# An adaLN block with linear attention and a token-mixing MLP: q's shift row is made from a folded sum in one matmul, an iteration later

## The chip, the cores and the metric

The kernel runs on one core of one Trainium2 chip. The metric is the device time of one execution in microseconds, taken as the median of several runs; the kernel before took 433.37 us (three runs, 433.33 to 433.41). All lines named L... are lines of the kernel before, unless the text says "after".

## The reference

Only the part that the change touches is shown; x has 2048 rows (tokens) of D = 448 channels, there are 16 heads of 28 channels, everything is float32.

```python
mod = (silu(c) @ w_mod).reshape(6, 448)
sa, ca, ga, sb, cb, gb = mod
h = layernorm(x) * (1 + ca) + sa
qkv = h @ wqkv                       # q, k, v: (2048, 448) each
phi = lambda t: where(t > 0, t + 1, exp(t)) + 1e-6
kv = sum over tokens of phi(k)^T v;  z = sum over tokens of phi(k)
o = phi(q) @ kv / (phi(q) @ z + 1e-6)          # per head
x = x + ga * (o @ wo)
h = layernorm(x) * (1 + cb) + sb
x = x + gb * transpose(gelu(transpose(layernorm(h)) @ w1 + b1) @ w2 + b2)
```

## The kernel before, in words

The 2048 tokens are cut into NT = 16 tiles of 128. Phase A computes k, phi(k), the sums over tokens, and some of the q's; phase B makes the attention's output and the MLP's first product; phase C the second. The change lies in phase A alone.

**Two-part numbers.** TensorE's fast type is a rounded float (F32R), so a float32 operand is split into a high part (ScalarE copies it into F32R) and a low part (VectorE, or a GpSimd transfer that adds, makes the rest), and a product is the sum of high x high, high x low and low x high.

**q and k without a normalised x.** For j = 0 (q) and j = 1 (k), the weights are multiplied by (1 + ca) per channel (Whi and Wlo, `w_high` L260 and `w_low` L272). x itself is used unnormalised, transposed (hh and hl, L411 and L415). The mean and the shift sa come in through two rows of each matrix: the negative column sum of the scaled weights, which is multiplied by a token's mean, and the row sa @ W, which is multiplied by its standard deviation (the spread is divided out later, in the exponent's scale). Both rows are rows of the tile Wrow[j] from partition 64 up, each in a high and a low part; `close(t, j)` (L439) ends a tile's product with one matmul over them. So no q can be closed before q's Wrow[0] is complete.

**How the row is made.** `row_part(0, ch)` (L278, L280) sums sa * W over four chunks of channels into accb, 128 partitions x 448, on VectorE. `row_sum(0)` (L287) lays the column sums of seven weight tiles into a PSUM tile rowb with seven F32R matmuls with the selector sel_s. `row_bias(0)` (L290) adds accb's sum over partitions with one matmul with the selector sel_b; accb and sel_b are plain float32, which the profile records as two matmuls. `row_out(0)` takes rows 64 to 97 out of PSUM on ScalarE (L294) and makes the low parts on VectorE (L295). The same is done for k (j = 1) far earlier.

**The loop and its order.** The order on each engine is the order in which the code issues: there is no reordering, each engine has its own queue and waits in it for what it needs. The loop `for t in range(4, NT)` (L682) is one iteration for each token tile: TensorE projects tile t + 1 for k, closes tile t, adds tile t - 4 into the sums of phi(k)^T x (`a_outer`, cacc, L554), transposes two tiles' mean and deviation rows on odd t (`a_transpose`, rw, L404), and from t = 10 on projects a q tile (`a_q`, L432 and L439 with the name qp). ScalarE and VectorE follow with the exponentials (L446, L449), the copies of the transposed rows (`a_copy`, L407), the splits and the norms (L496, L500, L505, L506). `a_pk_parts` (L527, L528) makes the low part of phi(k) for most tiles by a copy on ScalarE and an accumulating GpSimd transfer; `sum_end` (L541) issues another accumulating transfer. GpSimd's pow (L352) makes the deviations. SyncE's queue loads the tiles. In the kernel before, row_sum(0) and row_bias(0) stand in iteration 9 behind the close of tile 9, and row_out(0) at that iteration's end.

The modulation vectors use a like step: `mod_add(j)` (L237) folds partitions 64 to 111 onto the first ones, `mod_high(j)` (L242, L243) splits the folded 64 partitions into one tile, high part in partitions 0 to 63 and low part in 64 to 127.

Work tiles of phase A come from one ring of 74 slots (`slot`): each new tile takes the place of an old one and waits until that has been read.

Of the kernel before, what the change touches and what calls it, by code (L numbers as in the profile page):

```python
# [8 lines left out]
F32 = mybir.dt.float32  # L9
F32R = mybir.dt.float32r  # L10
AF = mybir.ActivationFunctionType
ALU = mybir.AluOpType
AX = mybir.AxisListType

P = 128
S, D, F = 2048, 448, 1792
# [15 lines left out]
ROWS = 98  # L32
# [19 lines left out]
def block_kernel(ctx: ExitStack, tc: tile.TileContext, x, xt, wqkv, wo, w1, b1, w2, c, wmod, wfirst, out):  # L52
    nc = tc.nc
# [5 lines left out]
    cst = ctx.enter_context(tc.tile_pool(name="cst", bufs=1))  # L59
# [16 lines left out]
    def moving(new, name, dt=F32R, parts=P):  # L76
        return new(name, dt=dt, parts=parts, w=512)[:, 16:16 + D]

    def bank(name):
        return psum.tile([P, 512], F32, name=name, tag="bank")  # L80
# [19 lines left out]
        nc.gpsimd.affine_select(out=m3, in_=m3, compare_op=ALU.is_ge, fill=0.0, base=DH - 1,  # L100
                                pattern=[[0, 4], [DH, 4], [0, DH]], channel_multiplier=-1)

    cst.tile([P, 112], F32, name="space")
    mhalf = cst.tile([P, 2], F32, name="mhalf")
    nc.vector.memset(mhalf, -0.5)
    roots = cst.tile([P, 2], F32, name="roots")
# [2 lines left out]
    sel_b = cst.tile([P, ROWS], F32, name="sel_b")  # L109
# [3 lines left out]
    for i in (64, 66, 96):  # L113
        nc.gpsimd.memset(sel_f[:, i:i + 1], -1.0)
        nc.gpsimd.memset(sel_b[:, i + 1:i + 2], 1.0)
    sel_s = cst.tile([P, ROWS], F32R, name="sel_s")
    rowst = []
    for i in range(RING):
        rowst.append(cst.tile([P, P], F32R, name=f"rowst{i}"))
# [115 lines left out]
    def mod_add(j):  # L235
        acc = macc[j]
        nc.vector.tensor_add(acc[:G - 64], acc[:G - 64], acc[64:])  # L237

    def mod_high(j):
        acc, both = macc[j], moving(slot, f"mh{j}")  # L240
        macc[j] = (both,)
        nc.scalar.activation(both[:64], acc[:64], AF.Copy)  # L242
        return lambda: nc.vector.tensor_sub(both[64:], acc[:64], both[:64].bitcast(F32))  # L243
# [12 lines left out]
    Whi, Wlo, Wrow, rowb, accb = {}, {}, {}, {}, {}  # L256
# [26 lines left out]
    def row_sum(j):  # L283
        rowb[j] = bank(f"rowb{j}")
        ws = [Whi[j, ch] for ch in range(4)] + [Wlo[j, ch] for ch in range(3)]
        for i, w in enumerate(ws):
            nc.tensor.matmul(rowb[j][:ROWS, :D], sel_s, w, start=(i == 0), stop=False)  # L287

    def row_bias(j):
        nc.tensor.matmul(rowb[j][:ROWS, :D], sel_b, accb.pop(j), start=False, stop=True)  # L290

    def row_out(j):
        ps, w = rowb.pop(j), Wrow[j]
        nc.scalar.activation(w[64:ROWS], ps[64:ROWS, :D], AF.Copy)  # L294
        nc.vector.tensor_sub(w[96:ROWS], ps[96:ROWS, :D], w[96:ROWS].bitcast(F32))  # L295
# [105 lines left out]
    def a_transpose(t):  # L401
        ps = bank(f"rw{t}")
        tps[t], tps[t + 1] = ps[:ROWS - 64, :P], ps[64:ROWS, :P]
        nc.tensor.transpose(ps[:ROWS, :P], rowst[t // 2 % RING][:, :ROWS].bitcast(F32), ident)  # L404
# [29 lines left out]
    def project(t, j, name):  # L434
        projects([(t, kind, ch) for ch in range(3) for kind in ("hh", "wl", "hl")] + [(t, "hh", 3)], j, name)

    def close(t, j):
        ps = pps.pop((t, j))
        nc.tensor.matmul(ps[:, :D], heads[t][1][:ROWS, 384:], Wrow[j][:ROWS], start=False, stop=True)  # L439
        return ps[:, :D]  # L440
# [10 lines left out]
    def a_exp(t, ps):  # L451
        a_exp1(t, ps)
        a_relu(t, ps)
# [22 lines left out]
    def a_q(t):  # L476
        project(t, 0, "qp")
        qps[t] = close(t, 0)
        del heads[t]
# [5 lines left out]
    def a_phi_q(keep=0):  # L485
        a_exp_q(keep)
        for t in sorted(eqs):
            pq[t] = phi_q(t)
# [24 lines left out]
    def a_pk_high(t):  # L513
        pks[t] = (moving(slot, f"pkh{t}"), moving(slot, f"pkl{t}"))
        nc.scalar.activation(pks[t][0], pkf[t], AF.Copy, bias=1e-6)

    def a_pk_parts(t):
        if t not in pks:
            a_pk_high(t)
        a_pk_low(t)  # L520

    def a_pk_low(t):
        pk, (hi, lo) = pkf.pop(t), pks[t]
        if t in DVE_LOW:
            nc.vector.scalar_tensor_tensor(lo, pk, 1e-6, hi.bitcast(F32), op0=ALU.add, op1=ALU.subtract)
        else:
            nc.scalar.activation(lo, hi.bitcast(F32), AF.Copy, scale=-1.0, bias=1e-6)  # L527
            nc.gpsimd.dma_start(lo, pk, accum_op=ALU.add)  # L528
        if t < 2:
            pksum.append(pk)  # L530
        elif t in SUM_DMA:
            late_sum.append((pksum[t % 2], pk))
        else:
            nc.vector.tensor_add(pksum[1], pksum[1], pk)
# [10 lines left out]
    def a_outer(t):  # L545
        if not cacc:
            cacc.extend(bank(f"cacc{ch}") for ch in range(4))
        xh, xl = xss.pop(t)
        kh, kl = pks.pop(t)
        for ch in range(4):  # L550
            s = slice(ch * P, (ch + 1) * P)
            todo = [(xh, kh), (xh, kl)] + ([(xl, kh)] if ch < 3 else [])
            for i, (a, b) in enumerate(todo[::1 if t > 1 else 2]):
                nc.tensor.matmul(cacc[ch][:, :D], a[:, s], b, start=(t == 0 and i == 0),  # L554
                                 stop=(t == NT - 1 and i == len(todo) - 1))
        if t < 2:
            for ch in range(4):
                nc.tensor.matmul(cacc[ch][:, :D], xh[:, ch * P:(ch + 1) * P], kl, start=False, stop=False)
# [121 lines left out]
    wo_sb = []  # L680
    late = [t for t in range(NT) if t not in Q_EARLY.values()]
    for t in range(4, NT):  # L682
        if 5 < t < NT - 1:
            project(t + 1, 1, "kp")
        kp = close(t, 1) if t > 4 else kps[4]
        if t == 9:
            row_sum(0)
            row_bias(0)
        if t > 4:
            a_outer(t - KV_LAG)  # L690
        if t % 2 and 4 < t < NT - 2:
            a_transpose(t + 1)
        if t in Q_EARLY:
            a_q(Q_EARLY[t])
        if t == 12:
            mp = mod_sum2(2)
        pair = t % 2 and 7 < t + 3 < NT
        if pair:
            first, second, end = a_stats_dve((t + 3, t + 4))
            first(0)  # L700
        if 5 <= t < 9:
            w_low(0, t - 5)
        if pair:
            second(0)
        if 5 <= t < 9:
            row_part(0, t - 5)
        a_phi_q(t in Q_EARLY)
        if t == 9:
            a_exp(t, kp)
        if t % 2 and 4 < t < NT - 2:  # L710
            a_copy(t + 1)
            a_copy(t + 2)
        if t != 9:
            a_exp(t, kp)
        if 7 < t + 3 < NT:
            a_split_high(t + 3)
        a_pk_parts(t - 1)
        highs = HIGH_AT.get(t, (t - 2,))
        for i in highs[:1]:
            a_norm(i)  # L720
            a_high(i)
        if t % 2 == 0 and 4 < t < NT - 3:
            low = a_rows(t + 2)
        if t == 11:
            low2 = mod_high(2)
        for j, i in MOD_AT.get(t, ()):
            mod_add(j) if i is None else mod_part(j, i)
        if t == 14:
            low4()
        a_pk(t, kp)  # L730
        if t % 2 == 0 and 4 < t < NT - 3:
            low()
        if 7 < t + 3 < NT:
            a_split_low(t + 3)
        for i in highs[1:]:
            a_norm(i)
            a_high(i)
        if pair:
            first(1)
        for i in highs:  # L740
            a_low(i)
        if pair:
            second(1)
            end()
        sum_end()
        if 4 <= t < 8:
            w_high(0, t - 4)
            if t == 7:
                w_row(0)
        if t == 9:  # L750
            row_out(0)
        if t == 12:
            mod_out(2, mp)
            make_mask()
        if t in FETCH:
            load_xt(FETCH[t])
            load_x(FETCH[t])
        if 7 <= t < 11:
            mod_part(2, t - 7)
        if t == 10:  # L760
            mod_add(2)
        if t == 11:
            low2()
        if t == 13:
            low4 = mod_high(4)
        if t in (7, 10):
            load_mod(4 if t == 7 else 3)
        if t == 10:
            load_qkv(2, tslot)
        if t == 8:  # L770
            for g in range(4):
                w = tslot(f"wo{g}", parts=G)
                nc.sync.dma_start(w, wo[g * G:(g + 1) * G, :])
                wo_sb.append(w)
            b12 = cst.tile([P, NF + NT], F32, name="b12")
            nc.sync.dma_start(b12, b1)
            b1c, b2c = b12[:, :NF], b12[:, NF:]
        if t >= 13:
            nc.vector.tensor_mul(wo_sb[t - 13], wo_sb[t - 13], mods[2][:G])
        load_to(PRE_LOAD.get(t, 0))  # L780
# [34 lines left out]
    for ch in range(4):  # L815
        for g in range(4):
            s = slice(g * G, (g + 1) * G)
            nc.tensor.matmul(kvb[:G, s], raw_w[2, ch][:, s], csum[ch][:, s], start=(ch == 0 and g == 0),  # L818
                             stop=(ch == 3), skip_group_check=True)
# [168 lines left out]
    for i in range(NT + LAG):  # L988
# [11 lines left out]
        t = i - LAG  # L1000
# [292 lines left out]
    for o0, n in W1G[1:]:  # L1293
# [5 lines left out]
        for r in range(first, NT):  # L1299
# [5 lines left out]
            if xleft:  # L1305
                t = xleft.pop(0)
# [80 lines left out]
```

## Time and profile before

| | |
|---|---|
| median of three runs | 433.37 us (433.33 to 433.41) |
| the profiled execution | 434.09 us, span 432.4 us |
| granted clock of TensorE | 1.00 |
| TensorE busy | 427.9 us, 99% of the span |
| VectorE, ScalarE, GpSimd busy | 365.1, 278.9, 120.1 us |
| DMA between 44 and 72 us | full (a share of 1.00 of the 16 engines), 240 GB/s |

The profile is one execution. In its lists an operation is named by the tile that it writes and those that it reads (out<-in); "idle before" is the time that its engine stood just before it, with what ended the wait. A matmul's 0.36 us is its whole way through the array; matmuls that follow each other start every 0.20 us, which the chain of work shows. The iteration with t = 9 lies between about 46 and 58 us: on TensorE its last matmuls end at 53.5 us, on VectorE its last operation starts at 57.42 us.

### The profile page before, as it was taken

How to read it: one execution, taken by the hardware profiler on the slowest of the kernel's cores; microseconds unless marked ns; L12 is line 12 of the kernel's file. 1: busy time of each engine (PE TensorE's matmuls, PEld its weight loads, DVE VectorE, ACT ScalarE, POOL GpSimd, SP SyncE). 2: the span in 40 equal slices, each digit the busy share in tenths (PEclk: the TensorE clock that was granted, in tenths of full speed). 3: DMA queues.
4: the chain of work that ended last, by engine and by line, in shares of the span. 5: the costliest groups of instructions: out<-in, count | busy, mean ns of one | idle time of the engine just before them, and what ended most of it. 6: DMA issues, size and time to landing. Idle time of an engine off the chain costs nothing.

```text
span 432.4 us, 7216 instructions
## 1 busy us (share of the span) xinstructions
PE 427.9 (99%) x2331; PEld 398.0 (92%) x2331; DVE 365.1 (84%) x814; ACT 278.9 (65%) x595; POOL 120.1 (28%) x199
## 2 busy tenths in 40 slices
PE   8999999999999999999999999999999999999997
PEld 8888899999899999999999999999999999999996
DVE  4899987889899999998579695739799998898894
ACT  5799869658578899996755263537464664655550
POOL 4345444300026577775200000010113131132010
PEclk9999999999999999999999999999999999999999
DMA  8997997565300036354427461577379977986431
GB/s 282 385 337 162 239 264 162 89 206 193 86 1 0 26 74 148 74 125 97 145 85 244 142 212 50 166 203 210 79 193 214 207 159 159 214 170 144 85 46 41
DMA packets 63797, 66.14 MB, mean 153 GB/s; under 512 B 4816, under 2 KB 55312, under 8 KB 63760
## 3 DMA queue, kind: packets, MB, share of 16 engines
q1 hardware_dynamic: 54688, 50.90, 37.8%
q0 software_dynamic: 8784, 14.32, 20.8%
q10 hardware_dynamic: 288, 0.46, 0.4%
q8 instruction: 18, 0.29, 0.3%
q14 instruction: 19, 0.16, 0.1%
HBM read 46.30 MB, written 7.34 MB: 124 GB/s over the span
## 4 chain that ended last, share of the span: by engine, by line
PE 97%; DVE 1%; ACT 1%; issue 0%
PE y L1183 19%; PE up L951 10%; PE up L950 10%; PE up L952 10%; PE y L1184 9%; PE cacc L554 7%; PE qp L432 7%; PE op L893 7%; PE kp L432 6%; PE op L900 1%; PE warm L188 1%; PE tq L863 1%; PE qp L439 1%; PE kvb L818 1%; PE wp L968 1%; PE rowb L287 1%
## 5 line engine op out<-in xcount | busy, mean ns | idle before, releaser
L950 PE MATMUL up<-h2h,ph 128*128 128x448 f32 x224 | 81.2, 362 | 0.0
L951 PE MATMUL up<-h2l,ph 128*128 128x448 f32 x224 | 81.2, 362 | 0.0
L952 PE MATMUL up<-h2h,pl 128*128 128x448 f32 x224 | 80.8, 361 | 0.0
L1138 POOL DMA_DIRECT2D a<-a x16 | 14.2, 964 | 142.6 <-DMA pr<-in_B_w_dram 76.7
L950 PEld LDWEIGHTS up<-h2h,ph 128*128 128x128 f32 x224 | 42.0, 188 | 3.1
L952 PEld LDWEIGHTS up<-h2h,pl 128*128 128x128 f32 x224 | 41.9, 187 | 3.0
L951 PEld LDWEIGHTS up<-h2l,ph 128*128 128x128 f32 x224 | 42.0, 188 | 2.3
L84 DVE TENSOR_TENSOR pl<-pr,ph 128x512 fp32r<-128x512 f32 x46 | 30.7, 688 | 2.6 <-ACT ph L83 1.7
L1189 ACT ACTIVATE cc<-y 128x448 f32<-128x448 f32 x24 | 13.0, 546 | 26.7 <-PE y L1184 26.7
L1102 DVE TENSOR_TENSOR u<-u,mod 128x448 f32<-128x448 f32 x14 | 8.7, 623 | 23.0 <-ACT u L1101 22.8
L83 ACT ACTIVATE ph<-pr 128x512 fp32r<-128x512 f32 x46 | 27.6, 623 | 0.8 <-PE up L952 0.5
L1101 ACT ACTIVATE u<-up,b 128x448 f32<-128x448 f32 x14 | 8.8, 625 | 25.4 <-PE up L952 24.9
L432 PE MATMUL kp<-wh,hh 128*128 128x448 f32 x64 | 23.8, 377 | 0.0
L554 PE MATMUL cacc<-pkh,xh 128*128 128x448 f32 x64 | 23.6, 369 | 0.0
L432 PE MATMUL qp<-wh,hh 128*128 128x448 f32 x64 | 23.5, 368 | 0.0
L1203 POOL DMA_DIRECT2D out_dram<-yt x14 | 12.7, 909 | 37.3 <-DVE yt L1194 27.9
L843 POOL TENSOR_SCALAR den<-den 128x16 f32<-128x16 f32 x16 | 8.8, 548 | 44.2 <-DVE den L840 44.2
L554 PE MATMUL cacc<-pkl,xh 128*128 128x448 f32 x56 | 20.3, 362 | 0.0
L893 PE MATMUL op<-wph,pth 128*128 128x448 f32 x48 | 18.7, 390 | 0.0
L1144 DVE TENSOR_TENSOR a<-a,s 128x512 f32<-128x512 f32 (+1 forms) x32 | 18.5, 622 | 0.0
L83 ACT ACTIVATE s2h<-s 128x512 fp32r<-128x512 f32 (+1 forms) x16 | 8.3, 569 | 15.5 <-DVE s L1144 15.5
L1183 PE MATMUL y<-ub,a11h 128*128 128x448 f32 x56 | 18.2, 375 | 0.0
(235 smaller groups left out, 1383.7 us busy)
## 6 DMA issues: line engine op xcount, KB each, us to landing
pr<-in_B_w_dram SPq DMA_DIRECT2D x56, 256.0 KB, 3.1
a<-in_B_w_dram SPq DMA_DIRECT2D x32, 256.0 KB, 4.8
a<-in_B_w_dram SPq DMA_DIRECT2D x32, 192.0 KB, 4.7
xt<-in_xt_dram SPq DMA_DIRECT2D x16, 256.0 KB, 5.0
x<-in_A_x_dram SPq DMA_DIRECT2D x16, 224.0 KB, 5.0
wm<-in_B_wmod_dram SPq DMA_DIRECT2D x16, 196.0 KB, 5.2
out_dram<-x SPq DMA_DIRECT2D x14, 224.0 KB, 2.3
out_dram<-yt POOLq DMA_DIRECT2D x14, 224.0 KB, 6.1
```

The source lines that it names most:

```text
L83: nc.scalar.activation(hi, full, AF.Copy)
L84: nc.vector.tensor_sub(lo, full, hi.bitcast(F32))
L432: nc.tensor.matmul(pps[t, j][:, :D], a[:, ch * P:(ch + 1) * P], w, start=first, stop=False)
L554: nc.tensor.matmul(cacc[ch][:, :D], a[:, s], b, start=(t == 0 and i == 0), stop=(t == NT - 1 and i == len(todo) - 1))
L893: nc.tensor.matmul(opb[t][:, :D], a, b, start=(ch == n == 0), stop=False)
L950: nc.tensor.matmul(ps[:, :D], hi[:, sl], mh, start=first, stop=False)
L951: nc.tensor.matmul(ps[:, :D], hi[:, sl], ml, start=False, stop=False)
L952: nc.tensor.matmul(ps[:, :D], lo[:, sl], mh, start=False, stop=last)
L1138: nc.gpsimd.dma_start(w, a, accum_op=ALU.add)
L1144: nc.vector.tensor_tensor(w, raw2[q, a][i], raw2[q, b][i], op=op)
L1183: nc.tensor.matmul(ps[:, :D], h[:, s], w, start=opens and r == 0, stop=False, skip_group_check=True)
L1184: nc.tensor.matmul(ps[:, :HD], l[:, s], wh, start=False, stop=closes and r == PAIRS - 1, skip_group_check=True)
```

## The change

q's row (j = 0) is made in another way; k's is left as it was.

- In iteration 9, behind `a_pk_parts(8)`, a GpSimd transfer adds accb's upper 64 partitions onto its lower 64 (`accum_op` add, 64 x 448).
- At the end of iteration 9, where row_out(0) stood, the new `row_fold(0)` copies sel_b into an F32R tile sel_r (ScalarE), copies the folded sum into the lower half of a new tile rb0 (ScalarE), and writes the low part into its upper half (VectorE).
- row_sum(0) and row_bias(0) go from iteration 9, behind the close of tile 9, to the very start of iteration 10. row_bias(0) takes sel_r and rb0, both F32R, in one matmul. row_out(0) goes to behind the close of tile 10.
- mod_add(2) goes from the end of iteration 10 to iteration 11, just ahead of mod_high(2).
- The tile "space" gives up the columns that sel_r takes. rb0 is one slot more in the ring.

```diff
-    cst.tile([P, 112], F32, name="space")
+    cst.tile([P, 14], F32, name="space")
...
+    sel_r = cst.tile([P, ROWS], F32R, name="sel_r")
...
     def row_bias(j):
-        nc.tensor.matmul(rowb[j][:ROWS, :D], sel_b, accb.pop(j), start=False, stop=True)
+        nc.tensor.matmul(rowb[j][:ROWS, :D], sel_r if j == 0 else sel_b, accb.pop(j), start=False, stop=True)
+
+    def row_fold(j):
+        acc, both = accb[j], moving(slot, f"rb{j}")
+        nc.scalar.activation(sel_r, sel_b, AF.Copy)
+        nc.scalar.activation(both[:64], acc[:64], AF.Copy)
+        nc.vector.tensor_sub(both[64:], acc[:64], both[:64].bitcast(F32))
+        accb[j] = both
...
     for t in range(4, NT):
+        if t == 10:
+            row_sum(0)
+            row_bias(0)
         if 5 < t < NT - 1:
             project(t + 1, 1, "kp")
         kp = close(t, 1) if t > 4 else kps[4]
-        if t == 9:
-            row_sum(0)
-            row_bias(0)
+        if t == 10:
+            row_out(0)
...
         a_pk_parts(t - 1)
+        if t == 9:
+            nc.gpsimd.dma_start(accb[0][:64], accb[0][64:], accum_op=ALU.add)
...
         if t == 11:
+            mod_add(2)
             low2 = mod_high(2)
...
         if t == 9:
-            row_out(0)
+            row_fold(0)
...
-        if t == 10:
-            mod_add(2)
```

What the order looks like now, engine by engine. First TensorE's queue before, from the close of tile 9 (kp9) on: rowb0 is q's row, wh0 and wl0 the seven weight tiles, cacc the sums that a_outer(5) adds to.

```order
L439 MATMUL kp9_733<-wrow1_280,hl9_630 128x448
L287 MATMUL rowb0_806<-wh0_0_534,sel_s_100 98x448
L287 MATMUL rowb0_806<-wh0_1_593,sel_s_100 98x448
L287 MATMUL rowb0_806<-wh0_2_650,sel_s_100 98x448
L287 MATMUL rowb0_806<-wh0_3_715,sel_s_100 98x448
L287 MATMUL rowb0_806<-wl0_0_558,sel_s_100 98x448
L287 MATMUL rowb0_806<-wl0_1_622,sel_s_100 98x448
L287 MATMUL rowb0_806<-wl0_2_681,sel_s_100 98x448
L290 MATMUL rowb0_806<-accb0_561,sel_b_90 98x448
L554 MATMUL cacc0_437<-pkh5_632,xh5_701 128x448
```

The same engine in the kernel after, with its own line numbers, from the last matmul of a_outer(5) to the first of iteration 10's projection of tile 11 (kp11); rw10 is the transpose of tile 10's and 11's rows.

```order
L562 MATMUL cacc3_441<-pkl5_634,xh5_702 128x448
L412 MATMUL rw10_818<-ident_78,rowst2_106 98x128
L288 MATMUL rowb0_865<-wh0_0_535,sel_s_100 98x448
L288 MATMUL rowb0_865<-wh0_1_594,sel_s_100 98x448
L288 MATMUL rowb0_865<-wh0_2_651,sel_s_100 98x448
L288 MATMUL rowb0_865<-wh0_3_716,sel_s_100 98x448
L288 MATMUL rowb0_865<-wl0_0_559,sel_s_100 98x448
L288 MATMUL rowb0_865<-wl0_1_623,sel_s_100 98x448
L288 MATMUL rowb0_865<-wl0_2_682,sel_s_100 98x448
L291 MATMUL rowb0_865<-rb0_856,sel_r_101 98x448
L440 MATMUL kp11_874<-wh1_0_223,hh11_763 128x448
```

The eight matmuls of q's row have moved behind a_outer(5) and the transpose, and the last of them reads rb0 instead of accb0; kp11 stands right behind it.

Next ScalarE's queue in the kernel after, at the end of iteration 9: pkl8 and xh7 are the last operations of that iteration ahead of row_fold(0), ek10 the first exponential of iteration 10.

```order
L523 ACTIVATE pkh8_834<-pk8_777 128x448
L535 ACTIVATE pkl8_835<-pkh8_834 128x448
L508 ACTIVATE xh7_842<-xn7_840 128x448
L295 ACTIVATE sel_r_101<-sel_b_90 128x98
L296 ACTIVATE rb0_856<-accb0_562 64x448
L302 ACTIVATE wrow0_718<-rowb0_865 34x448
L454 ACTIVATE ek10_911<-kp10_795,mv10_678 128x448
```

Before, wrow0 (L294) stood directly behind xh7 (L500); now sel_r and the copy of the folded accb0 stand between them.

Last GpSimd's queue in the kernel after, around the new transfer: pkl7 and pkl8 are transfers of `a_pk_parts`, pk1 and pk0 those of `sum_end`, mv12 the pow.

```order
L536 DMA pkl7_767<-pk7_705 128x448
L549 DMA pk1_453<-pk7_705 128x448
L536 DMA pkl8_835<-pk8_777 128x448
L729 DMA accb0_562<-accb0_562 64x448
L360 TENSOR_TENSOR mv12_820<-ve12_821,roots_87 128x2x2
L549 DMA pk0_400<-pk8_777 128x448
```

The transfer of accb0 stands directly behind that of pkl8, so it is issued no earlier than that one, and mv12 comes one place later. On VectorE the subtraction that writes rb0's low half takes the place that wrow0's subtraction (L295) had, behind ve12; wrow0's comes two places later, behind acc2.

## The prediction

> **What bounds the kernel now.** I read the first page of the profile, then TensorE's waits, then the chain of work that ended last, and last each engine's instructions in order of time around iteration 9 of the loop over token tiles, where all of the change lies.
>
> ```profile
> PE 427.9 (99%) x2331; PEld 398.0 (92%) x2331; DVE 365.1 (84%) x814; ACT 278.9 (65%) x595; POOL 120.1 (28%) x199
> ...
> PE 97%; DVE 1%; ACT 1%; issue 0%
> ```
>
> TensorE is busy for 427.9 of 432.4 us and carries 97% of the chain. Its waits are two in all:
>
> ```profile
> PE warm L188 <- DVE roots L108: 1.1, 1, 1.1
> PE rw L404 <- ACT rk L449: 0.2, 1, 0.2
> ```
>
> One lies at the start and one early; behind iteration 9 it waits for nothing. So a microsecond of matmuls taken away should be a microsecond off the end, and a microsecond in which TensorE stands still should be one added, since no later wait takes it back. How large such a payback could be at most is in the rivals.
>
> The chain in order of time (start, length, engine and line, count) shows the place:
>
> ```profile
> 48.86 0.20 PE kp L439
> 49.06 1.42 PE rowb L287 x7
> 50.48 0.75 PE rowb L290 x2
> 51.23 2.22 PE cacc L554 x11
> 53.45 0.11 PE rw L404
> 53.56 2.01 PE kp L432 x10
> ```
>
> These rows are the matmuls' steps from start to start (0.20 us for 448 columns); the 0.36 us that the groups give for one matmul overlap. q's row is seven matmuls of 0.20 us and the one with accb, which stands as two records of 0.375 us. TensorE starts iteration 10 (kp of tile 11) at 53.56.
>
> **Part 1, the gain: one pass instead of two records.** The new matmul's operands are of the rounded type that the seven have. Its record should cost what theirs do, 0.20 us: 0.75 - 0.20 = 0.55 us less on TensorE. If the two records stayed, it would be 0; nothing in the profile prices it below 0.20 us. I take 0.55 us.
>
> **Part 2, the move: when TensorE needs the row, and when it is there.** In the new order a_outer(5) and the transpose follow tile 9's close at once, then the seven, then the row matmul. That is 49.06 + 2.22 + 0.11 + 1.42 = 52.81 us: TensorE then stands before the row matmul and needs both halves of rb0. Before, it needed only accb, whose last sum started at 49.01 (below). VectorE's and ScalarE's queues lag behind it at this place, as their rows in order of time say (start, length, operation, [idle before, and its releaser]):
>
> ```profile
> 49.01 0.69 DVE L280 SCALAR_TENSOR_TENSOR accb<-wr,col,accb 128x448 f32<-128x448 f32 x1
> ...
> 53.27 0.48 DVE L496 TENSOR_SCALAR xn<-x,mv 128x448 f32<-128x448 f32 x1
> ...
> 54.85 0.69 DVE L415 TENSOR_TENSOR hl<-xt,hh 128x512 fp32r<-128x512 f32 x1 [0.56 <-ACT hh L411]
> ...
> 56.40 0.23 DVE L505 TENSOR_TENSOR xh<-xn,xh 128x64 fp32r<-128x64 f32 x1 [0.32 <-ACT xh L500]
> ...
> 57.42 0.63 DVE L295 TENSOR_TENSOR wrow<-rowb,wrow 2x448 fp32r<-2x448 f32 x1
> ```
>
> The subtraction that makes the low half takes the very place of the last of these rows, at the end of VectorE's iteration 9: 57.42 us. Even if all of VectorE's idle time in the stretch goes (0.56 + 0.32 us), it starts at 56.54. It should last as long as the like one of mod_high, 64 x 448:
>
> ```profile
> 70.06 0.62 DVE L243 TENSOR_TENSOR mh<-acc,mh 64x448 fp32r<-64x448 f32 x1
> ```
>
> So by VectorE's place alone the row is there at 57.16 at the earliest, 4.35 us after TensorE asks. That is the lower end for the wait.
>
> **Part 3, the transfer before it.** In front of this subtraction ScalarE copies the folded sum, and the fold is a GpSimd transfer queued behind pkl of tile 8:
>
> ```profile
> 51.15 0.63 ACT L449 ACTIVATE rk<-kp,mv 128x448 f32<-128x448 f32 x1
> 53.59 0.57 ACT L407 ACTIVATE hl<-rw 34x128 fp32r<-34x128 f32 x2 [1.82 <-PE rw L404]
> ...
> 55.32 0.58 ACT L527 ACTIVATE pkl<-pkh 128x448 fp32r<-128x448 f32 x1
> 55.80 0.56 ACT L500 ACTIVATE xh<-xn 128x448 fp32r<-128x448 f32 x1
> 56.39 0.54 ACT L294 ACTIVATE wrow<-rowb 34x448 fp32r<-34x448 f32 x1
> ...
> 68.91 0.56 ACT L242 ACTIVATE mh<-acc 64x448 fp32r<-64x448 f32 x1
> ```
>
> ```profile
> 56.30 0.88 POOL L528 DMA_DIRECT2D pkl<-pk  x1 [3.45 <-ACT pkl L527]
> ...
> 73.57 0.86 POOL L528 DMA_DIRECT2D pkl<-pk  x1 [1.12 <-ACT pkl L527]
> 74.12 1.23 POOL L541 DMA_DIRECT2D pk<-pk  x1
> ```
>
> The transpose now comes 2.17 us earlier (1.42 + 0.75 moved from ahead of it), so ScalarE loses its 1.82 us of waiting at L407, and no more, since rk ends at 51.78. Its pkl ends at 55.90 - 1.82 = 54.08; GpSimd's issue follows 0.40 us later as before, at 54.48. The next issue comes 0.55 us behind it, as in the pair at 73.57 and 74.12: the fold is issued at about 55.0. From issue to landing this queue's two kinds of accumulating transfer took, between 30 and 80 us of the span, first pkl, then the sums:
>
> ```profile
> DMA to landing us min/median/max: 3.2/4.4/6.5
> ```
>
> ```profile
> DMA to landing us min/median/max: 3.2/5.2/7.3
> ```
>
> The fold moves half as much as each of these. It runs right behind another on the same queue, while the stretch's DMA is full, so I go by the medians: 4.7 us, landed at 59.7. Ends: 3.2 us (58.2) and 7.3 us (62.3).
>
> ScalarE reaches the copy at about 54.8 (xh ends at 56.36 - 1.82 = 54.54, and sel_r's copy of 98 columns costs a part of mh's 0.56 us; it ends long before the landing). It then stands until 59.7. Copy 0.56, subtraction 0.62, and 0.2 us for the three hand-overs: TensorE goes on at 61.1. It starts kp of tile 11 at 61.3 instead of 53.56: **+7.7 us**, the 0.55 us of part 1 already in it (a wait of 8.3). Ends +6.2 and +10.3.
>
> **Who stands behind these waits.** On ScalarE: wrow0, ek10, rk10 and tile 13's split. On VectorE: acc2, wrow0's low row, xn8, the rows for tile 12. On GpSimd: the pow for mv12, one issue later. None of it becomes a second wait of TensorE: VectorE reaches xn8 near 62.9 instead of 58.69 (4.2 late), and TensorE, which wants all of this, is 7.7 us late. Loads on SyncE that wait for TensorE's or ScalarE's buffers slip by the same. The two small moves, mod_add(2) (0.62 us of VectorE) into iteration 11 and one slot more in the ring, lie beside TensorE's work: 0; without that cover, at most their 0.62 us.
>
> **Part 4, TensorE's pace after standing still.** The profile's granted clock is 1.00 throughout, but the start shows a slow pace: the chain's step for a full-precision record of 128 columns there, beside one of 448 columns later, and the first kp matmuls:
>
> ```profile
> 1.11 2.93 PE warm L188 x12
> ...
> 108.81 3.01 PE wp L968 x8
> ```
>
> ```profile
> 9.17 0.72 PE L432 MATMUL kp<-wh,hh 128*128 128x448 f32 x1
> 9.69 0.53 PE L432 MATMUL kp<-wh,hl 128*128 128x448 f32 x1
> 10.06 0.37 PE L432 MATMUL kp<-wl,hh 128*128 128x448 f32 x1
> 10.27 0.37 PE L432 MATMUL kp<-wh,hh 128*128 128x448 f32 x1
> ```
>
> 2.93/12/128 = 1.9 ns a column against 3.01/8/448 = 0.84; and the kp steps go from 0.52 to 0.21 us at 10.06. TensorE began at under half its pace and kept it for 10.06 - 1.11 = 8.9 us. No row shows whether 8.3 us of standing in the middle brings that back. Ends: 0, and 8.9 us at half pace, which loses 4.5. Before the start it had stood still too, which is the nearer row, but there it was also fed unevenly; I take the middle, **2.2 us**.
>
> The Trainium skill (TensorE: Matmul & The Clock Gate, Part 1: The HAM clock gate) says that the array's clock halves after an idle window of about 3.4 us and comes back after about one busy window; the windows run freely. The trace agrees on the half pace at the start, though it lasts 8.9 us there. By the page the loss would be half of 3.4 to 6.8 us, 1.7 to 3.4, and the sum +9.4 to +11.1.
>
> **The sum.** +7.7 + 2.2 = +9.9 us. The profiled execution took 434.09 us, its span 432.4; the median of the runs is 433.37, 0.72 lower. The sum is a difference inside the span, so I put it on the median: 443.3 us.
>
> **The rivals.**
> - Full pace after the wait: part 3 holds, part 4 is 0. For it: the granted clock never falls on the page. Against: the start. 433.4 + 7.7 = 441.1 us. Chance 0.13. By the clock gate of the Trainium skill this would not happen after 8 us.
> - VectorE's place alone: the transfer lands by 55.3, so that only the subtraction's place counts. It would have to land within 0.3 us of its issue, or be issued at 52.1, before pkl of tile 8 is made. 57.16 + 0.05 + 0.20 - 53.56 = +3.85: 437.2 us, 439 at half pace. Chance 0.04.
> - Not slower: the stop is paid back. While TensorE stands, transfers and the other engines get ahead, and small gaps later close.
>
> ```profile
> 110.00:432.00 322.00, 319.34 (x1790) 299.76 (x1788) 271.22 (x590) 197.45 (x431) 82.70 (x138) 1.00 0.52 128
> ```
>
> Of the 322.00 us behind 110, TensorE is busy for 319.34 (its second number), so 2.7 us at most can be given back. With the 0.55 us of part 1 that covers a wait of 3.2 us: from there on the change is not slower. It would need rb0 done by 56.0, before VectorE's earliest 57.16. At a wait of 3.2 us it ends at 433.4. Chance 0.03.
> - That the change would not do what it says (two records still) moves the sum by 0.55 us and no sign.
>
> **How the numbers follow.** Forecast 0.80, the rivals 0.13, 0.04 and 0.03. The range 439.3 to 448.0 us: its low end is the early landing at full pace (433.4 + 6.2 = 439.6) with a little for the hand-overs, its high end the late landing at half pace for 8.9 us (433.4 + 10.3 + 4.5 = 448.2); it leaves out the second and third rival. A measurement of this kernel can tell about 0.2% (0.87 us) from no change; of the cases only the third rival comes near: faster 0.01, same 0.02, slower 0.97.
>
> **What would show it.** In the profile after: TensorE waiting for VectorE's rb ahead of L291, 8.3 us (7 to 11), between about 53 and 61; ScalarE waiting about 5 us for the transfer accb ahead of L296; that transfer landing 3.2 to 7.3 us after its issue; the row matmul one record of 0.36 us; kp steps of 0.4 us for some microseconds after it; no new wait of TensorE later. Wrong would be: no wait at L291, or one under 4 us (then part 2 misreads the engines' lag); a wait as said but an end less than 6 us later (then something gives it back); or a total more than 5 us over the wait (then the pace or a second stop costs more).

## The result, and the profile after

The kernel after took 445.32 us (median of five runs, 445.01 to 447.22) against 433.41 us for the kernel before beside it (five runs, 433.33 to 433.42): ratio 1.0289, 95% interval 1.0265 to 1.0313, or 11.9 us more. The profiled execution took 445.32 us with a span of 443.6. All lines named L... are now those of the kernel that the sentence speaks of.

The page of after, its first line, the engines' busy time, and the granted clock in 40 slices:

```profile
span 443.6 us, 7217 instructions
...
PE 431.1 (97%) x2330; PEld 397.2 (90%) x2330; DVE 365.9 (82%) x815; ACT 279.8 (63%) x597; POOL 121.0 (27%) x200
...
PEclk9999969999999999999999999999999999999999
```

TensorE has one record less than before and yet is busy 3.2 us longer (431.1 against 427.9), and the clock row has a 6 where before had none: the sixth slice, 55.5 to 66.5 us. The busy time hides the stop; TensorE's waits show it:

```profile
PE rowb L291 <- DVE rb L297: 8.1, 1, 8.1
PE warm L189 <- DVE roots L108: 1.1, 1, 1.1
```

The wait in front of it, from all engines' waits between 40 and 85 us:

```profile
ACT rb L296 <- DMA accb<-accb: 5.0, 1, 5.0
DVE rb L297 <- ACT rb L296: 3.7, 1, 3.7
```

The chain of work between 44 and 85 us (start, length, engine and line) has the whole of it in a row:

```profile
53.83 0.18 ACT sel_r L295
54.02 0.53 POOL pkl L536
54.55 4.44 DMA accb<-accb
59.01 0.58 ACT rb L296
59.59 0.02 issue
59.62 0.63 DVE rb L297
60.24 0.04 issue
60.29 0.69 PE rowb L291
60.98 3.48 PE kp L440 x10
64.46 0.20 PE kp L447
64.66 2.21 PE cacc L562 x11
66.87 2.04 PE qp L440 x10
```

The transfer is 4.44 us of it. The ten kp matmuls right behind the row take 3.48 us, where before they took 2.01; the next eleven take their usual 2.21. The last row is the beginning of something that the prediction has no step for: ten qp matmuls in 2.04 us, not 2.00. The granted clock of the same stretch, in windows of 2 us (window, its length, the busy time of PE, PEld, DVE, ACT and POOL, then granted clock, DMA share, GB/s):

```profile
54.00:56.00 2.00, 0.00 (x0) 0.00 (x0) 1.87 (x6) 0.01 (x1) 1.76 (x3) 1.00 1.10 282
56.00:58.00 2.00, 0.00 (x0) 0.00 (x0) 0.00 (x0) 0.00 (x0) 1.90 (x2) 0.80 1.08 183
58.00:60.00 2.00, 0.00 (x0) 0.00 (x0) 0.39 (x1) 0.58 (x1) 0.00 (x0) 0.50 0.79 134
60.00:62.00 2.00, 1.71 (x5) 1.56 (x6) 1.33 (x3) 0.54 (x1) 0.00 (x0) 0.50 0.28 90
62.00:64.00 2.00, 2.00 (x7) 1.80 (x6) 0.82 (x3) 0.00 (x0) 0.00 (x0) 0.50 0.87 275
64.00:66.00 2.00, 2.00 (x11) 1.87 (x11) 0.05 (x1) 1.24 (x3) 0.00 (x0) 1.00 0.23 85
```

The 0.80 means full clock to 57.2 and half from there. TensorE had stopped at 52.2 (60.29 less 8.11, the wait in order of time); at 64.0 the clock is full again. Between 56 and 58 only GpSimd is busy in this row: TensorE, VectorE and ScalarE stand for one transfer.

**Where the 11.9 us are.** The rows account for the first part: the wait 8.11, the row matmul 0.69 instead of 0.75 (-0.06), the kp matmuls 3.48 instead of 2.01 (+1.47), together 9.52. For the rest I set the start of each matmul in after against the start of the same matmul in before. The difference is -0.63 at 48.8 us of before's span (the slow pace at the start ended sooner in this execution: the 14 warm matmuls there take 1.83 us, before's 3.36), 8.88 at 58 us, and 11.27 at 429 us. So 9.51 us come at the row, as the rows say, and **2.39 us come later**, in small steps without any wait of TensorE. The experiments had to find what these are.

### The profile page after: what moved, and what is told of

Same layout as the page of the kernel before. It is cut to its first block, busy times and chain, and to the rows that moved or that the text cites. A ratio compares the mean times of both kernels' runs of the same rounds, so it can differ in the third digit from the quotient of the medians.

```text
span 443.6 us, 7217 instructions
## 1 busy us (share of the span) xinstructions
PE 431.1 (97%) x2330; PEld 397.2 (90%) x2330; DVE 365.9 (82%) x815; ACT 279.8 (63%) x597; POOL 121.0 (27%) x200
## 4 chain that ended last, share of the span: by engine, by line
PE 86%; DMA 5%; DVE 5%; ACT 2%; issue 1%; POOL 0%; ACTq 0%
PE y L1194 18%; PE up L961 10%; PE up L963 10%; PE up L962 10%; PE y L1195 9%; PE qp L440 7%; PE op L904 7%; PE cacc L562 5%; PE kp L440 3%; DMA xt<-in_xt_dram 2%; DMA wr<-in_qkv_dram 2%; PE op L911 1%; PE tq L874 1%; DMA accb<-accb 1%; DVE hl L423 1%; PE qp L447 1%
## 5 line engine op out<-in xcount | busy, mean ns | idle before, releaser
L1194 PE MATMUL y<-ub,a12h 128*128 128x448 f32 x56 | 18.2, 374 | 0.0
```

The costliest lines, as they stand in the source:

```text
L1194: nc.tensor.matmul(ps[:, :D], h[:, s], w, start=opens and r == 0, stop=False, skip_group_check=True)
```

## The experiments

The same difference sorts all kernels, so its change over the row (from 48.8 to 58 us of before's span; to 60 us in e1, where other matmuls stand around 58) and behind the row (from there to 429 us) stands here for each. "Before" is the kernel before's median beside it on the same chip. Each has one profiled execution.

| kernel | us | before | ratio, 95% interval | at the row | behind it |
|---|---|---|---|---|---|
| after | 445.32 | 433.41 | 1.0289 [1.0265, 1.0313] | +9.51 | +2.39 |
| e1_row_late | 443.14 | 433.75 | 1.0219 [1.0201, 1.0237] | +7.02 | +2.35 |
| e2_fold_vector | 442.93 | 433.75 | 1.0208 [1.0194, 1.0222] | +6.08 | +2.41 |
| e3_filled | 444.43 | 433.75 | 1.0245 [1.0231, 1.0259] | +7.74 | +2.40 |
| e4_early | 436.68 | 433.75 | 1.0062 [1.0048, 1.0076] | +0.11 | +2.39 |
| f1_space8 | 443.70 | 433.60 | 1.0225 [1.0210, 1.0240] | +10.45 | -0.06 |
| f2_early_space8 | 433.61 | 433.60 | 0.9999 [0.9991, 1.0008] | +0.16 | -0.05 |
| f3_before_shift | 435.99 | 433.60 | 1.0054 [1.0041, 1.0066] | +0.05 | +2.41 |
| f4_move_only | 434.42 | 433.60 | 1.0011 [0.9999, 1.0023] | -0.01 | +1.25 |
| f5_after_hl | 435.29 | 433.77 | 1.0039 [1.0027, 1.0052] | -0.56 | +1.62 |
| f6_shift64 | 435.49 | 433.77 | 1.0040 [1.0028, 1.0052] | 0.00 | +1.68 |
| h1_fold_later | 433.17 | 433.57 | 0.9996 [0.9987, 1.0005] | -0.48 | -0.04 |
| h4_fold_later_mod | 433.10 | 433.57 | 0.9994 [0.9985, 1.0003] | -0.49 | 0.00 |

### The row asked for later (e1_row_late)

The row's matmuls go behind a_outer(6), and q's projection of iteration 10 to its end.

```diff
-        if t == 10:
-            row_sum(0)
-            row_bias(0)
...
         # behind a_outer(6)
+        if t == 10:
+            row_sum(0)
+            row_bias(0)
...
+        if t == 10:
+            a_q(Q_EARLY[t])
```

> The fold and its transfer stay; q's eight row matmuls, and with them the wait, stand behind a_outer(6) of iteration 10 instead of at its start, row_out(0) behind a_high. TensorE asks 4.4 us later (2.0 + 0.2 + 2.2 us of matmuls now stand ahead), and rb0 is ready when it was, since the transfer's place is the same. Theory 1 (the order alone: ready time minus asking time): a wait of 8.1 - 4.4 = about 3.8 us ahead of the row matmul, no half pace after so short a stop, so 433.4 + 3.8 - 0.55 = 436.6 us. Theory 2 (the new work and the shifted ring cost by themselves, also without a wait: the 2.3 us that TensorE's matmuls lose little by little between 66 and 430 us): 436.6 + 2.3 = 438.9 us.

It came out at 443.14 us, above both. TensorE had some 4.4 us more to do before it asked, and still waited 5.4 us, because the transfer came later. Waits of e1:

```profile
ACT rb L296 <- DMA accb<-accb: 6.8, 1, 6.8
...
PE rowb L291 <- DVE rb L297: 5.4, 1, 5.4
```

Its transfer was issued at the same 54.55 us and landed 6.3 us later, against 4.4 in after. From the list of what the tile accb does in e1:

```profile
DMA to landing us min/median/max: 6.3/6.3/6.3
```

And from the same list of after:

```profile
DMA to landing us min/median/max: 4.4/4.4/4.4
```

The windows of e1 between 58 and 62 us, in the columns of after's above, say what differs:

```profile
58.00:60.00 2.00, 0.00 (x0) 0.00 (x0) 0.00 (x0) 0.00 (x0) 0.00 (x0) 0.84 1.09 303
60.00:62.00 2.00, 0.00 (x0) 0.00 (x0) 0.57 (x1) 1.16 (x3) 0.00 (x0) 0.50 1.03 229
```

The DMA share is 1.09 and 1.03 where after has 0.79 and 0.28: in after the loads ran dry while TensorE stood, here they went on beside the fold. That the loads go on because TensorE frees their buffers is argued from this, not tried. Half clock came here too, after 2.7 us of standing.

### VectorE folds (e2_fold_vector)

The transfer's line becomes an addition on VectorE at the same place of the code.

```diff
-            nc.gpsimd.dma_start(accb[0][:64], accb[0][64:], accum_op=ALU.add)
+            nc.vector.tensor_add(accb[0][:64], accb[0][:64], accb[0][64:])
```

> Only the transfer is replaced: VectorE adds the upper half of accb to the lower one at the same place in its own queue, as mod_add does (0.62 us). Theory 1: ScalarE's copy no longer waits, and the row is ready by VectorE's place alone, about 57.0 us in the after trace's time; TensorE asks at 51.9: a wait of about 5.1 us instead of 8.1, so 3 us less; the clock may or may not drop at that length, 0 to 1.7 us. 433.4 + 5.1 - 0.55 = 438.0, up to 439.7 us. Theory 2: 2.3 us on top of that, 440.3 to 442.0. If the transfer was not what ended the wait, nothing changes: 445.3.

TensorE's waits of e2:

```profile
PE rowb L291 <- DVE rb L297: 4.9, 1, 4.9
```

That is the one wait of TensorE behind the start over 0.2 us. The prediction's part 2 had 4.35 us for VectorE's place alone; with 0.62 us for the added operation it is 4.97. In after, VectorE stood 3.7 us before the subtraction: of the 8.1 us the transfer and the copy behind it make 3.7, VectorE's place 4.4. Half clock came as well; the row and the matmuls behind it in e2's chain:

```profile
57.95 0.69 PE rowb L291
58.64 3.29 PE kp L440 x10
```

That is (0.69 - 0.20) + (3.29 - 2.01) = 1.77 us, and with the wait 4.9 - 0.55 + 1.77 = 6.1 us, the table's +6.08. Its clock was at half for one period of 3.4 us, and at the full pace again by 61.3.

### The wait filled with matmuls (e3_filled)

40 matmuls whose result is not used write the row's PSUM tile ahead of its seven, the first of which starts the sum anew.

```diff
+        for i in range(fill):
+            nc.tensor.matmul(rowb[j][:ROWS, :D], sel_s, Whi[j, 0], start=True, stop=True)
...
-            row_sum(0)
+            row_sum(0, 40)
```

> The changed kernel with 40 more matmuls of 0.20 us (8 us) in rowb ahead of row_sum(0), whose first matmul starts the sum afresh, so that TensorE works through its stop. The row is ready when it was. Theory 1 with part 4 of the prediction (the pace after standing still): the first matmuls after the row start every 0.20 us instead of every 0.37, and the kernel is 1.4 to 1.8 us shorter than the change: about 443.6 us. If the slow residue between 66 and 430 us comes from the stop of the clock too, another 2.3 us go: 441.3. If the pace had nothing to do with standing still: 445.3, with half pace as before.

The chain of e3 from the row (L293) on; the fillers, 8.07 us of L287, and the seven stand just ahead:

```profile
61.12 0.40 PE rowb L293
61.51 2.05 PE kp L442 x10
63.57 0.21 PE kp L449
63.78 2.21 PE cacc L564 x11
```

TensorE doesn't wait there, the clock is 1.00 throughout, and the ten kp matmuls take 2.05 us instead of 3.48. So the half pace in after comes of standing still, not of the row or its operands. The drift behind the row, 2.40 us, is still there: it has nothing to do with the stop.

### Everything early (e4_early)

VectorE folds in iteration 8, row_fold stands in iteration 9 behind the exponentials, and the row's matmuls stand behind the close of tile 10 (before had them behind that of tile 9).

```diff
+        # t == 8, behind the low parts of the next tiles' rows
+            nc.vector.tensor_add(accb[0][:64], accb[0][:64], accb[0][64:])
...
+        # t == 9, behind the exponentials
+            row_fold(0)
...
+        # t == 10, behind the close
+            row_sum(0)
+            row_bias(0)
```

> The one-matmul row with its parts made in time: VectorE folds accb in iteration 8 behind the row casts, row_fold(0) stands behind the exponentials of tile 9, and TensorE asks for the row behind the close of tile 10 (row_out(0) right behind it). Theory 1: rb0 is ready near 53, TensorE asks at about 54.2 in the after trace's time, no wait, and only part 1 is left: 433.4 - 0.55 = 432.9 us, with 0.2 us for small waits at the transposes. Theory 2: the new work and the ring cost by themselves, 432.9 + 2.3 = 435.2 us.

TensorE no longer waits for the row, and the kernel is still 2.9 us slower than before: +0.11 at the row and the full +2.39 behind it. A row made in time costs almost nothing; the drift remains, alone. The row matmul itself takes the forecast 0.20 us, as the chain of f2 shows, the same kernel with the tiles in before's places:

```profile
54.99 0.20 PE rowb L291
```

In the total nothing is to be seen of the 0.55 us, since a new wait takes most of it (TensorE's waits of e4):

```profile
PE kp L440 <- DVE hl L423: 0.4, 1, 0.4
```

The fold stands ahead of hl11 on VectorE, and TensorE wants hl11 for iteration 10's projection.

### Where the tiles lie: f1_space8, f2_early_space8, f3_before_shift, f6_shift64

The tile "space" had 112 columns, 448 bytes of each partition. In after it has 14, 56 bytes that are rounded up to 64, and sel_r has 98 columns, 392 rounded up to 416: together 480. All tiles laid out behind them lie 32 bytes further. f1 is after, f2 is e4, with the 32 bytes taken back; f3 is before with nothing but the shift; f6 shifts it by 64.

```diff
 # f1 (from after) and f2 (from e4_early)
-    cst.tile([P, 14], F32, name="space")
+    cst.tile([P, 8], F32, name="space")
 # f3 (from before)
-    cst.tile([P, 112], F32, name="space")
+    cst.tile([P, 120], F32, name="space")
 # f6 (from before)
-    cst.tile([P, 112], F32, name="space")
+    cst.tile([P, 128], F32, name="space")
```

> The changed kernel, with 8 columns instead of 14 in the unused tile space, so that space and sel_r together take the 448 bytes a partition that space took before (in the change they take 480: 56 + 392 bytes, each rounded up to 32). All tiles behind them, those of the pool tok with q's and k's weights among them, lie where they lay before; in the change they lie 32 bytes further. Theory 3 (address): the matmul steps of 0.204 to 0.205 us, which in the change and in all four variants replace many of 0.201 us, come from these 32 bytes. Then 3 us or a little more go (2.3 us behind 66 us and near 1 us between 11 and 46): 445.3 - 3.3 = 442.0 us; the wait of 8.1 us and the half pace stay. Theory 2 (the fold's work or the slot in the ring): 445.3 as the change.

> The variant whose row is ready in time, with 8 columns in space as well. Theory 3: no step of 0.205 us that was not there before, and only part 1 of the prediction is left: 433.4 - 0.55 = 432.9 us, up to 433.2 with small waits. Theory 2: 436.7 as without the 8 columns. If the row's new work costs as well as the address, between them.

> The kernel before with 120 instead of 112 columns in the unused tile space, and nothing else: the same instructions in the same order, every tile behind space 32 bytes further, as in the change. Theory 3: about 3.3 us slower, 436.7 us, with steps of 0.204 to 0.205 us in the k, q and op matmuls. Theory 2: 433.4 us, no change.

> The kernel before with 128 instead of 112 columns in the unused tile space: everything behind it lies 64 bytes further, instead of 32 as in the change and in the run that cost 2.4 us. If what costs is the place within 64 bytes, 433.6 us and no more steps of 0.205 us than before; if it is the distance or that the tiles moved at all, about 436.

f3 does the same instructions as before in the same order, waits no more, and takes 2.4 us longer; f1 and f2 have no drift. The ten matmuls of one q tile far behind the row show it. In the chain of after:

```profile
121.54 2.06 PE qp L440 x10
```

In f3's, before with 32 bytes more:

```profile
111.86 2.06 PE qp L432 x10
```

In f1's, after with the 32 bytes taken back:

```profile
121.80 2.01 PE qp L440 x10
```

In f6's, before with 64 bytes more:

```profile
112.24 2.04 PE qp L432 x10
```

Each matmul of the slower ones starts 0.205 or 0.206 us (in f6 0.204) behind the one before it instead of 0.201. Of the 2.4 us in after and f3, 1.85 come so between 60 and 200 us, from the matmuls of the q's, the attention's output and a part of the MLP's first product; at 4.5 ns each that is an estimated 400 matmuls. The other 0.5 us come behind 300 us, in the second product. So the drift is the place of the tiles, shown from both sides. Which operand's place counts is open: the eleven cacc matmuls, both of whose operands are tiles of the ring, take 2.20 to 2.22 us in before, f3 and f6 alike, while the slower kp, qp and op read a tile of another pool beside one of the ring. A shift by 64 bytes, f6, costs 1.68 us, so it is not the place within 64 bytes alone; that it is how the places of a matmul's two operands stand to each other is a guess that wasn't tried.

f1 gives the stop without the shift, the case that the prediction worked out: 443.70 against 433.60, +10.1 us. It stood 8.3 us and had three periods of 3.4 us at half clock instead of two, hence +10.45 at the row in its profile. f1's windows, the first two and the one in which the clock comes back:

```profile
54.00:56.00 2.00, 0.00 (x0) 0.00 (x0) 1.77 (x6) 0.00 (x0) 1.77 (x3) 0.87 1.11 289
56.00:58.00 2.00, 0.00 (x0) 0.00 (x0) 0.00 (x0) 0.00 (x0) 1.81 (x2) 0.50 1.12 195
...
64.00:66.00 2.00, 2.00 (x8) 1.77 (x7) 0.00 (x0) 0.78 (x2) 0.00 (x0) 0.57 0.31 116
```

By these shares the clock is half from 55.5 to 65.7 us. TensorE had worked again for 2.0 us when the second period ended, at 62.3, and got a third.

### The move without the fold (f4_move_only)

accb and sel_b are used as before, sel_r is left out and "space" has its 112 columns again; only the row's matmuls, row_out and mod_add stand where after has them.

```diff
 # f4 (from after)
-            nc.gpsimd.dma_start(accb[0][:64], accb[0][64:], accum_op=ALU.add)
...
-            row_fold(0)
...
-        nc.tensor.matmul(rowb[j][:ROWS, :D], sel_r if j == 0 else sel_b, accb.pop(j), start=False, stop=True)
+        nc.tensor.matmul(rowb[j][:ROWS, :D], sel_b, accb.pop(j), start=False, stop=True)
```

> One part of the change alone: the row matmuls go to the start of iteration 10 and row_out(0) behind the close of tile 10, mod_add(2) into iteration 11, but accb is used as before, in full precision with sel_b, without fold, transfer, sel_r or rb0; space has its 112 columns. Theory 1: TensorE asks at about 52.8 for accb, which has been ready since 49.7: no wait, 433.4 us, within 0.3 us. If asking an iteration later costs by itself (row_out on the path of the first q's close, ScalarE behind it), some tenths to 2 us more.

The move costs nothing at the row (-0.01 us), as accb is long there. But it costs 1.25 us later. TensorE's wait and its releaser's, of f4:

```profile
ACT rq L472 <- DMA pk<-pk: 4.2, 1, 4.2
...
PE qp L438 <- ACT rq L472: 1.0, 1, 1.0
```

The releaser is the sum transfer (pk<-pk), which reads pk8 and takes 6.4 us to land. Why rq of the first q waits for it is argued: accb is read by the late row matmul and so gives its slot back later, the tiles behind it in the ring get other slots, and rq gets pk8's. No row shows the slots themselves. In the medians this is +0.8 us, with an interval that touches no change; the wait in the trace is plain.

### The fold behind hl (f5_after_hl), and further (h1_fold_later, h4_fold_later_mod)

f5 is f2 with the fold three operations later on VectorE and row_fold behind the copies of the rows; h1 is f2 with the fold moved behind hl11's making and no more; h4 is h1 with mod_add(2) back at the end of iteration 10.

```diff
 # h1 (from f2_early_space8)
-            if t == 8:
-                nc.vector.tensor_add(accb[0][:64], accb[0][:64], accb[0][64:])
...
+        if t == 8:
+            nc.vector.tensor_add(accb[0][:64], accb[0][:64], accb[0][64:])
 # h4 (from h1)
-            mod_add(2)
...
+        if t == 10:
+            mod_add(2)
```

> The variant with 8 columns in space and the row in time, its fold on VectorE three operations later: behind tile 11's hl and tile 7's high and low parts instead of ahead of them (before, kp of tile 11 waited 0.5 us for hl), and row_fold(0) behind the copies of the transposed rows. If part 1 of the prediction is right and only VectorE's 0.62 us of folding stood on TensorE's path, that wait goes, TensorE's start-to-start time over iterations 9 and 10 is 0.55 us shorter than before (it was 0.16 longer with the wait), and the kernel takes 433.0 us against 433.6 of before on this chip. If the gain of one matmul is not there at all, 433.6.

> As the run in which VectorE folds in iteration 8 and nothing is moved in the tiles' places (433.61), but the fold stands behind the making of hl11, so that tile 11's projection no longer waits for it; the tile rb0 and the ring's order stay as there. Theory (TensorE's own queue sets the time; the row's one pass gives 0.55 us, and only queue places and slots eat it): no wait of TensorE behind the start longer than 0.3 us, offset behind the row -0.5, total 0.5 us under the kernel before beside it: 433.1 if that is 433.6. Rival (the ring's slots or another engine's lateness take it back wherever the fold stands, as in both earlier tries): a new wait of 0.5 to 1.6 us between 58 and 80 us and a total equal to before or up to 1 us over it.

> As the run beside it, with the sum for the modulation vector left where the kernel before has it, at the end of iteration 10. By the prediction's step that this move lies beside TensorE's work: the same time within 0.2 us. If the move matters, TensorE waits at the product with the modulation vector (before 80 us) in one of the two and not in the other, by up to 0.6 us.

f5 has the gain, -0.56 us over the row, and loses 1.62 us between 64 and 80 us. Its waits in that stretch:

```profile
DVE acc L231 <- DMA pk<-pk: 4.7, 1, 4.7
...
PE modp L254 <- DVE mh L244: 1.4, 1, 1.4
```

It looks like f4's mechanism once more: the next sum for a modulation vector gets a slot that a transfer still reads (this one takes 8.5 us to land), VectorE stands before it, and the product with the modulation vector comes late.

h1 has neither. All of TensorE's waits in h1, then its chain at the row:

```profile
PE warm L189 <- DVE roots L108: 1.1, 1, 1.1
PE rw L412 <- ACT rk L457: 0.2, 1, 0.2
PE kp L440 <- ACT wh L261: 0.2, 1, 0.2
```

```profile
52.95 1.41 PE rowb L288 x7
54.36 0.30 PE rowb L291
54.66 2.20 PE cacc L562 x11
```

0.30 us stand where before had 0.75, and nothing takes it back: -0.48 at the row, -0.04 behind it. The medians, 433.17 and 433.10 against 433.57, say the same size, but both intervals hold 1: by the times alone these two versions cannot be told from before, by the trace they are 0.5 us shorter. mod_add(2)'s place makes no difference between h1 and h4. The rival, that the ring or another engine takes the gain back wherever the fold stands, falls by these two traces.

## Why the prediction was right, and what it left out

It said 443.3 us (439.3 to 448.0) and slower; the chip said 445.32. The 2.0 us between come of one term that it lacks (+2.4) and two that were a little high (0.1 and 0.2). Without that term, in f1, the kernel is 10.1 us slower, where the sum said 9.9. That the total still fell into the range is owed to the width that the pace and the landing gave it, not to an allowance for the missing term.

- **Part 1, the gain: right.** The row matmul takes 0.20 us in f2 and 0.30 in h1. f5 shows -0.56 us over the row and h1 -0.48, against -0.55. In after it is swallowed: the row matmul's 0.69 us there is a pass at half clock.
- **Part 2, VectorE's place: right.** After's 8.1 us less VectorE's 3.7 leave 4.4 against 4.35. e2, without the transfer, waits 4.9 us where 4.35 and 0.62 make 4.97.
- **Part 3, the transfer: right.** Landing 4.4 us (4.7 said), the wait 8.1 (8.3 said), the net 8.11 - 0.55 = 7.56 us (7.7 said). ScalarE stood 5.0 us for it, as forecast. Its reason held only by half: "the stretch's DMA is full" is so up to 58 us, and then it runs dry, by the argument at e1 because TensorE stands. In e1, where it stays full, the same transfer took 6.3 us. The three hand-overs, 0.2 us in the sum without a row behind it, take about 0.1 in the chain.
- **Part 4, the pace: right in kind, its size partly luck.** (0.69 - 0.20) + (3.48 - 2.01) = 1.96 us against 2.2; e3 shows the cause. But 2.2 was the middle between nothing and a half pace of 8.9 us, as at the start, counted from the moment TensorE goes on. The windows of after show the clock at 0.50 from 57.2 to 64.0, 6.8 us, of which the first 3.1 fell on the stop; and the 8.9 us were one execution's, after's own start ran at full pace from about 6 us. The Trainium skill (TensorE: Matmul & The Clock Gate, Part 1: The HAM clock gate) has windows of about 3.4 us that run freely; the runs agree: half clock lasted 6.8 us in after and e1, 3.4 in e2, 10.2 in f1, whole numbers of 3.4, and began 2.7 to 5.0 us after TensorE stopped. The idle window that the prediction has from the Trainium skill does not hold to the letter: in e1 TensorE worked in the first 0.7 of the 3.4 us ahead of the fall. That the same stop costs one window more or less by how they fall fits two of after's five runs, 446.8 and 447.2 us with a mean clock of 0.988 and 0.989, beside the others at 445.0 to 445.3 with 0.991.
- **"The two small moves ... 0": right here, but not a rule.** mod_add(2)'s move costs nothing (h1 and h4), and f1, f2 and h1, all with rb0's slot more, lose nothing behind the row. Without TensorE's delay the prediction allowed at most 0.62 us, and that bound is too low: when tiles of the ring come free at other times, f4 (which has no rb0) and f5 lose 1.25 and 1.62 us before a transfer that still runs.
- **The step that failed is one that wasn't made.** The diff's first line, 112 columns of "space" to 14, was described and never priced. It looks like bookkeeping, but 14 and 98 columns don't fill 112 once each tile is rounded up, and 32 bytes cost 2.39 us (2.41 in f3, where nothing else changed).

Of the rivals, full pace after the wait falls to the clock rows; e3 is what it would look like. VectorE's place alone falls to the 4.4 us landing; e2 shows its wait, though with the added operation, half clock and the shift it ends at 442.9, not 437.2. That the stop is paid back falls plainly: behind the row the difference to before shrinks by 0.06 us at most (f1). The two records became one.

## What to carry to other kernels

A transfer between engines that is short in bytes is long in a chain: issue, 4 to 6 us here to the landing and three hand-overs, and TensorE's clock is charged on top; put it where its result is wanted some ten microseconds later (f5's slowest took 8.5), or fold on an engine that has room. When an operand's making moves, look at what its release moves in the ring: the wait turns up at another tile, far behind. And when a diff changes a tile's size, compare the addresses of everything behind it before believing that the rest is unchanged; one run of the old kernel with only the shift prices it.

## What the runs showed of the hardware that was not expected

- A shift of the tiles by 32 bytes in each partition costs 2.4 us, most of it as 2% on an estimated 400 matmuls; by 64 bytes, 1.7 us. No wait shows it, nor the clock (1.00 in e4, which has the whole drift); only the step from start to start does.
- Half clock does not need a long stop: e2's 4.9 us and e1's 5.4 us brought it, at 1.8 and 2.1 us (in e1 the ten matmuls behind the row take 3.63 us). In e2 it set in 0.1 us before TensorE went on, so that nearly all of it fell on work.
- Two microseconds of work do not bring the clock back at once: in f1 it stayed at half for one more period of 3.4 us.
